# Row loads of the decay issued by GpSimd, and the first 500 places of a written order replaced

## The chip, the cores and the metric

The kernel runs on one NeuronCore of a Trainium2 chip. The metric is the device time of one execution in microseconds, as the median of several executions. TensorE multiplies matrices into PSUM; VectorE, ScalarE and GpSimd work on SBUF (VectorE and ScalarE on PSUM too); SyncE, called SP, only issues DMA. In the profile these engines are PE (with PEld, its weight loads), DVE, ACT, POOL and SP.

## The reference

A forgetting attention, whose result is the input of a gated feed-forward block with a convolution:

```python
# q, k, v: (8 batches, 8 heads, 576, 64); f: (8, 8, 576)
scores = np.matmul(q, k.transpose(0, 1, 3, 2)) / np.sqrt(64)
cum = np.cumsum(np.log(np.clip(f, 1e-4, 1.0)), axis=-1)
scores = np.where(causal, -1e9, scores + cum[:, :, :, None] - cum[:, :, None, :])
attn = softmax(scores)
x = matmul(attn, v)                     # brought to (8, 576, 512)
h = np.maximum(x @ w_in, 0.0)           # w_in: 512 x 1024
conv_out[s] = sum over k of conv_w[k] * h[s + k - 1]     # three taps along the sequence
out = (h / (1 + np.exp(-conv_out))) @ w_out              # w_out: 1024 x 512
```

## The kernel before

The attention is worked in 16 half batches of four heads (`hb` 0 to 15), each of two pairs of heads (`i` = 2 hb + p). The feed-forward block is worked by batch (`b` 0 to 7) and by eight slices of 128 hidden channels (`ff`). The program is a set of small steps, each with a name, an engine or a choice of engines, the steps it needs and the buffers that it takes and gives (`add`). They are issued in the order that the string `ORDER` (line 18) writes out, one place for each step; `@ACT` and the like after a name choose the engine. Each engine runs its own steps in that order, and PSUM buffers (four of them, `ps`) go round in that order as well. The names:

- `dca`, `dcl`, `dcs`, `dck`: the decay `f` is clipped, its logarithm taken (ScalarE), summed by a scan and scaled into the rows `kc` (VectorE). `ki` (line 278, `decay_image`): three DMA transfers write `kc` to an image in DRAM.
- `cw`, `cwt`: the convolution weights are turned on TensorE and made into ratios by seven small steps on VectorE.
- `ld`, `tp`, `cl` of half batches 0 and 1: q (side 0) and k (side 1) are loaded plainly, turned by TensorE (`turn_qk`, line 162, nine transposes) and copied from PSUM into the buffers `qk` by ScalarE or VectorE (`turned_qk`, line 168). Later half batches come with a transposing DMA of SP (`q2.0`, `q2.1` and so on, `load_qk`, line 177); for half batches 2 to 7 VectorE then clamps rows in place (`cl2.0` and so on, line 184).
- `rw1` to `rw7` (line 200, `rows_of`): two DMA transfers bring rows of the image into the q and k buffers of a half batch, so that the score product adds the decay. Half batch 0 adds it by extra matmuls instead (`by_matmul`); half batches 8 to 15 take it by `fi` (`fill`).
- `v`, `va`: v is loaded by SP in five parts for each batch and cast to 16 bits by POOL, ACT or DVE (`va2.0`: parts 0 to 3; `va2.1`: the last; lines 219 and 221).
- `sd`, `so`, `st`: score products on TensorE, of the diagonal blocks of a pair, of the blocks off the diagonal for one head, of the last 64 places for a half batch (line 314). `ed`, `eo`, `et`: their exponentials on ScalarE (lines 355, 372, 334). `sd`, `so` and `st` need the half batch's row loads.
- `pv`: the product with v on TensorE in two parts (lines 391 and 396), needing all exponentials and the cast v. `n`, `m`: reciprocal and scaling on VectorE (lines 405 and 407). `t`, `tx`: the result is turned on TensorE (line 416) and copied (line 419).
- `f`: product with `w_in` (line 431); `r`: relu on ScalarE (442); `c`, `d`: convolution on VectorE (448, 450); `a`: tanh on ScalarE (453); `g`: gate on VectorE (460); `o`: product with `w_out` (476); `e`, `s`: copy out and store. `wi`, `wo` and `wic`, `woc` load and cast the weights (line 520).

A DMA that SP issues waits in SP's order for what it needs, and all later ones behind it. Before the change `ki` and `rw1`, `rw2`, `rw3`, `rw6`, `rw7` are issued by SP and `rw4`, `rw5` by ScalarE.

Of the kernel before, what the change touches and what calls it, by code (L numbers as in the profile page):

```python
# [21 lines left out]
class Plan:  # L22
# [34 lines left out]
def kernel(  # L57
# [11 lines left out]
    nc = tc.nc  # L69
# [5 lines left out]
    BH = B * H  # L75
# [24 lines left out]
    image = dpool.tile([4, 2, BH, S], BF16, name="image")  # L100
# [45 lines left out]
    add = plan.add  # L146
# [53 lines left out]
    def rows_of(hb, e="SP"):  # L200
        dma = {"SP": nc.sync, "ACT": nc.scalar}[e].dma_start
        h0 = 2 * PAIRS if hb == 0 else 0
        c = slice(hb * HH + h0, (hb + 1) * HH)
        dma(even_rows(hb, 0, 1, h0 * S, HS), image[0:1, 0, c, :].rearrange("j h s -> j (h s)"))
        dma(even_rows(hb, 1, 2, HS + h0 * S, 2 * HS), image[1:3, 1, c, :].rearrange("j h s -> j (h s)"))
# [73 lines left out]
    def decay_image(e):  # L279
        for j, a, h in ((0, 0, 0), (1, 1, 0), (2, 1, 1)):  # L280
            {"SP": nc.sync, "ACT": nc.scalar}[e].dma_start(image[j, a], kc[BH * h:BH * (h + 1)])
# [256 lines left out]
    for hb in range(NHB):
        b = hb // 2
        was = hb - RING  # L540
        old = [f"st{was}"] + [f"sd{2 * was + y}" for y in range(2)] + [
            f"so{2 * was + y}.{s}" for y in range(2) for s in range(2)] if was >= 0 else []
        if hb < NPL:
            parts = [(p, side) for p in range(2) for side in range(2)]
            loads = [(p, 1, side) for p, side in parts] if hb == 0 else [(0, 2, side) for side in range(2)]
            add(f"ld{hb}", "SP", [], lambda: None, take=["he"])
            got = {}
            for p0, np, side in loads:
                n = add(f"ld{hb}.{p0}.{side}", "SP", [], lambda hb=hb, side=side, p0=p0, np=np: load_plain(hb, side, p0, np),
                        behind=[f"ld{hb}"])  # L550
                got.update({(p, side): n for p in range(p0, p0 + np)})
            for p, side in parts:
                add(f"tp{hb}.{p}.{side}", "PE", [got[p, side]], lambda hb=hb, p=p, side=side: turn_qk(hb, p, side),
                    take=["ps"], give=[("he", f"ld{hb}")] if (p, side) == (1, 1) else [],
                    behind=[f"tp{hb}.{x}.{y}" for x, y in parts] [:2 * p + side])
                add(f"cl{hb}.{p}.{side}", "DVE/ACT", [f"tp{hb}.{p}.{side}"] + old,
                    lambda e, hb=hb, p=p, side=side: turned_qk(hb, p, side, e), give=[("ps", f"tp{hb}.{p}.{side}")])
            if hb == 0:
                ready = [["dck"] + [f"cl0.{p}.{side}" for side in range(2)] for p in range(2)]
                if PAIRS < 2:  # L560
                    add("rw0", "SP", ["cl0.1.0", "cl0.1.1", "ki"] + ([] if PAIRS else ["cl0.0.0", "cl0.0.1"]), lambda: rows_of(0))
                    ready = [ready[p] if p < PAIRS else ["rw0"] for p in range(2)]
            else:
                add(f"rw{hb}", "ACT/SP", [f"cl{hb}.{p}.{side}" for p, side in parts] + ["ki"], lambda e, hb=hb: rows_of(hb, e))
                ready = [[f"rw{hb}"]] * 2
        else:
            for side in range(2):
                add(f"q{hb}.{side}", "SP", old, lambda hb=hb, side=side: load_qk(hb, 0, 4, side))
            if hb < NCL:
                for side in range(2):  # L570
                    add(f"cl{hb}.{side}", "DVE", [f"q{hb}.{side}"], lambda hb=hb, side=side: clamp(hb, 0, 4, side))
                add(f"rw{hb}", "ACT/SP", [f"cl{hb}.{side}" for side in range(2)] + ["ki"], lambda e, hb=hb: rows_of(hb, e))
                ready = [[f"rw{hb}"]] * 2
            else:
                add(f"fi{hb}", "SP", [f"q{hb}.0", f"q{hb}.1", "zc", "ki"], lambda hb=hb: fill(hb))
                ready = [[f"fi{hb}"]] * 2
# [43 lines left out]
    for b in range(B):  # L620
# [72 lines left out]
```

## Time and profile before

| | |
|---|---|
| median of three runs | 245.96 us (245.56 to 246.7) |
| the profiled execution | 247.66 us, of which the span of the trace is 245.9 |
| TensorE busy | 229.1 us (93%) |
| VectorE busy | 205.7 us (84%) |
| ScalarE busy | 207.2 us (84%) |
| GpSimd busy | 52.6 us (21%) |
| DMA | 49.68 MB |

The profile is of one execution. Its page has the busy time of the engines, the span in 40 slices, the DMA queues, the chain of waits that ended last, and the costliest groups of instructions. A row of the timeline has the start in us, the length, the engine, the line of the code, the operation, what it writes and reads, the count of instructions put together, and in brackets the idle time before it and what ended that. A matmul's end is modelled, so that rows of TensorE overlap; the distance from start to start is the step's price. Idle time of an engine that sets nothing costs nothing.

### The profile page before, as it was taken

How to read it: one execution, taken by the hardware profiler on the slowest of the kernel's cores; microseconds unless marked ns; L12 is line 12 of the kernel's file. 1: busy time of each engine (PE TensorE's matmuls, PEld its weight loads, DVE VectorE, ACT ScalarE, POOL GpSimd, SP SyncE). 2: the span in 40 equal slices, each digit the busy share in tenths (PEclk: the TensorE clock that was granted, in tenths of full speed). 3: DMA queues.
4: the chain of work that ended last, by engine and by line, in shares of the span. 5: the costliest groups of instructions: out<-in, count | busy, mean ns of one | idle time of the engine just before them, and what ended most of it. 6: DMA issues, size and time to landing. Idle time of an engine off the chain costs nothing.

```text
span 245.9 us, 6391 instructions
## 1 busy us (share of the span) xinstructions
PE 229.1 (93%) x2627; PEld 146.5 (60%) x2627; DVE 205.7 (84%) x323; ACT 207.2 (84%) x278; POOL 52.6 (21%) x77
## 2 busy tenths in 40 slices
PE   0899899959999999999999999999999999999992
PEld 0778676537655776666556865685576557444440
DVE  5626329899999899999999988996999889999951
ACT  2748695999999889999999999999988997698452
POOL 8020430004240030004130481156303131000000
PEclk9999999999999999999999999999999999999999
DMA  6999799999999899999989999929999780551426
GB/s 202 329 154 231 242 189 206 219 201 325 225 203 191 198 196 219 234 301 212 234 248 249 177 191 283 263 48 187 272 245 197 185 192 4 129 176 50 171 87 213
DMA packets 120280, 49.68 MB, mean 202 GB/s; under 512 B 109863, under 2 KB 110375, under 8 KB 120251
## 3 DMA queue, kind: packets, MB, share of 16 engines
q1 hardware_dynamic: 120073, 48.94, 89.1%
q8 instruction: 20, 0.33, 0.6%
q10 hardware_dynamic: 178, 0.34, 0.5%
q14 instruction: 9, 0.07, 0.1%
HBM read 21.11 MB, written 10.17 MB: 127 GB/s over the span
## 4 chain that ended last, share of the span: by engine, by line
PE 79%; DVE 7%; DMA 5%; ACT 5%; issue 1%; SPq 1%; ACTq 0%; DVEq 0%
PE ps L476 25%; PE ps L431 24%; PE ps L314 15%; PE ps L391 7%; DMA qk<-image 3%; DMA u<-in_f_dram 2%; PE ps L396 2%; PE ps L416 2%; PE ps L322 2%; ACT qk L172 2%; DVE xm L407 2%; DVE u L448 1%; DVE u L450 1%; PE ps L317 1%; PE ps L319 1%
## 5 line engine op out<-in xcount | busy, mean ns | idle before, releaser
L431 PE MATMUL ps<-xt,w_in_f 128*128 128x512 f16 (+1 forms) x512 | 70.1, 287 | 0.4 <-DVE xt L419 0.4
L372 ACT ACTIVATE pp<-ps 128x1024 f16<-128x1024 f32 x64 | 64.6, 1030 | 4.1 <-PE ps L314 2.3
L476 PE MATMUL ps<-w_out_f,hg 128*128 128x512 f16 x288 | 66.8, 380 | 0.0
L314 PE MATMUL ps<-qk 128*128 128x128 bf16 (+2 forms) x576 | 64.8, 242 | 1.3 <-ACT pp L355 0.7
L448 DVE SCALAR_TENSOR_TENSOR u<-ht,cwt 128x576 f32<-128x576 f16 x64 | 54.0, 860 | 3.9 <-ACT ht L442 3.6
L453 ACT ACTIVATE hg<-u,cw 128x576 f16<-128x576 f32 x64 | 48.6, 781 | 6.1 <-DVE u L450 6.0
L450 DVE SCALAR_TENSOR_TENSOR u<-ht,cwt,u 128x576 f32<-128x576 f16 x64 | 52.9, 841 | 0.5
L431 PEld LDWEIGHTS <-w_in_f 128*128 128x128 f16 x512 | 34.3, 98 | 28.7 <-issue 0.5
L314 PEld LDWEIGHTS <-qk 128*128 128x128 bf16 x576 | 39.7, 98 | 19.5 <-issue 3.5
L442 ACT ACTIVATE ht<-ps 128x576 f16<-128x576 f32 x64 | 40.9, 661 | 6.4 <-PE ps L431 3.0
L476 PEld LDWEIGHTS <-hg 128*128 128x128 f16 x288 | 26.9, 98 | 28.9
L460 DVE SCALAR_TENSOR_TENSOR hg<-hg,ht 128x576 f16<-128x576 f16 x51 | 38.8, 773 | 0.5 <-ACT hg L453 0.5
L358 POOL TENSOR_SCALAR_AFFINE_SELECT pp<-pd 128x1024 f16<-128x1024 f32 x16 | 19.7, 1245 | 54.2 <-ACT pd L355 54.2
L391 PE MATMUL ps<-va,pp 128*128 128x65 f16 x640 | 24.8, 193 | 1.7 <-DVE va L219 1.7
L391 PEld LDWEIGHTS <-pp 128*128 128x128 f16 x640 | 22.6, 97 | 4.2 <-DVE va L219 2.0
L407 DVE TENSOR_TENSOR xm<-ps,rc 128x896 f16<-128x896 f32 (+1 forms) x32 | 23.9, 752 | 0.5
L355 ACT ACTIVATE pp<-ps 128x1024 f16<-128x1024 f32 x16 | 16.5, 1034 | 5.8 <-PE ps L314 3.3
L355 ACT ACTIVATE pd<-ps 128x1024 f32<-128x1024 f32 x16 | 16.2, 1023 | 1.2 <-PE ps L314 0.5
L219 POOL CAST va<-vf 128x1024 f16<-128x1024 f32 x8 | 9.9, 1233 | 32.6 <-DVE u L448 18.3
L322 PE MATMUL ps<-mask,ident 128*128 128x512 bf16 (+1 forms) x40 | 14.8, 370 | 1.4 <-ACT pp L372 0.8
L405 DVE RECIPROCAL rc<-ps 128x14 f32<-128x14 f32 (+1 forms) x32 | 6.7, 209 | 10.1 <-PE ps L396 4.9
L481 ACT COPY ob<-ps 128x1024 f32<-128x1024 f32 (+1 forms) x14 | 12.9, 918 | 0.3 <-issue 0.2
(83 smaller groups left out, 180.2 us busy)
## 6 DMA issues: line engine op xcount, KB each, us to landing
vf<-in_v_dram SPq DMA_DIRECT2D x32, 256.0 KB
out_dram<-ob SPq DMA_DIRECT2D x14, 512.0 KB
qk<-blank SPq DMA_DIRECT2D x8, 432.0 KB
ob<-in_moe_w_in_dram SPq DMA_DIRECT2D x4, 512.0 KB
ob<-in_moe_w_out_dram SPq DMA_DIRECT2D x4, 512.0 KB
out_dram<-ob SPq DMA_DIRECT2D x6, 256.0 KB
vf<-in_v_dram SPq DMA_DIRECT2D x8, 128.0 KB
qk<-blank SPq DMA_DIRECT2D x8, 108.0 KB
```

Of the source, the lines that this page charges most:

```text
L314: nc.tensor.matmul(o, tk[:, h * S + k0:h * S + k0 + 128], tq[:, h * S + q0:h * S + q0 + n], start=first, stop=last and not by_matmul(hb, h))
L355: nc.scalar.activation(o, ps_of(f"sd{i}").rearrange("p (s c) -> p s c", s=2), AF.Exp, scale=SCALE)
L372: nc.scalar.activation(pair(i)[:, s, 512:1536], ps_of(f"so{i}.{s}"), AF.Exp, scale=SCALE)
L391: nc.tensor.matmul(ps[:, c:c + D + 1], block(hb, h, m, n), va[:, h, m, 0:D + 1], start=(m == 0), stop=(m == n))
L407: nc.vector.tensor_tensor(xm[:, CUT * D * u:CUT * D * u + nj * k * D].rearrange("p (j x d) -> p j x d", x=k, d=D), got[:, :, :, 0:D], r.un ...
L431: nc.tensor.matmul(ps[:, t0:t1], w_in_f16[:, cc, 128 * ff:128 * (ff + 1)], xt[:, cc // 2, x:x + t1 - t0], start=(cc == 0), stop=(cc == NCC ...
L442: nc.scalar.activation(ht_of(b, ff)[:, 2:2 + S], ps_of(f"f{b}.{ff}")[:, 0:S], AF.Relu, scale=1.0 if (b, ff) in LATE else 0.5)
L448: nc.vector.scalar_tensor_tensor(u, ht[:, 1:1 + S], cwt[:, ff, 0:1], ht[:, 2:2 + S], op0=ALU.mult, op1=ALU.add)
L450: nc.vector.scalar_tensor_tensor(u, ht[:, 3:3 + S], cwt[:, ff, 1:2], u, op0=ALU.mult, op1=ALU.add)
L453: nc.scalar.activation(hg_of(b, ff), u_t[slot[f"c{b}.{ff}", "u"]], AF.Sigmoid if (b, ff) in LATE else AF.Tanh, scale=cw[:, ff, 1:2])
L460: nc.vector.scalar_tensor_tensor(hv, hv, 1.0, ht_of(b, ff)[:, 2:2 + S], op0=ALU.add, op1=ALU.mult)
L476: nc.tensor.matmul(ps[:, 512 * (c % 2):512 * (c % 2 + 1)], w, w_out_f16[:, ff, :], start=(ff == 0), stop=(ff == NFF - 1))
```

## The change

`rows_of` and `decay_image` may be issued by GpSimd as well, and the first 500 of the 1054 places of the order are others; the last 554 are as they were. The same 1054 steps are done. In the new order

- `ki` is issued by ScalarE and `rw1` to `rw7` by GpSimd;
- other steps change engine: `cl0.1.0` and `cl1.0.0` go from ScalarE to VectorE and `cl1.0.1` the other way; `wic1`, `wic2`, `wic3` from GpSimd to ScalarE and `woc2` from GpSimd to VectorE; `tx1` from VectorE to ScalarE; the value casts `va1.0`, `va6.0` and `va6.1` from GpSimd to VectorE, `va4.0` and `va5.1` from ScalarE to VectorE, `va3.0`, `va7.1` and `va8.0` from ScalarE to GpSimd, `va7.0` from VectorE to GpSimd; the copy out `e1.1` from ScalarE to VectorE;
- `q4.1` comes behind the loads of batch 1's values (`v1`), as `q4.0` did;
- the four transposes of half batch 1 come directly behind `sd0`, and `pv0.0` comes behind half batch 1's first scores; the convolution ratios `cwt` come ahead of the scan `dcs`.

The order is one line in the file; here it is broken, and shown up to `f1.2`:

```diff
--- before.py
+++ after.py
 ORDER = """
-dca cw ld0 ld1 ld0.0.0 tp0.0.0 dcl ld0.1.0 ld0.0.1 tp0.0.1 tp0.1.0 v0.0 ld0.1.1 ld1.0.1 ld1.0.0 dcs
-dck v0.1 v0.2 v0.3 v0.4 va0.0@POOL ki@SP va0.1@POOL q2.1 cl0.0.0@ACT cl0.0.1@ACT cl0.1.0@ACT tp0.1.1
-q2.0 cwt sd0 ed0 cl0.1.1@DVE wi1 wic1@POOL so0.1 eo0.1 tp1.0.0 so0.0 eo0.0 tp1.0.1 cl1.0.0@ACT
-cl1.0.1@DVE sd1 ed1 va1.0@POOL va1.1@DVE tp1.1.0 tp1.1.1 cl1.1.1@ACT so1.1 eo1.1 so1.0 st0 eo1.0
-pv0.0 et0 cl1.1.0@DVE rw1@SP sd2 ed2 so2.1 eo2.1 st1 wi0 so2.0 sd3 wi2 wic0@POOL wi3 et1 eo2.0 cl2.0
-cl2.1 rw2@SP n0.0 m0.0 q3.0 q3.1 so3.1 wic2@POOL ed3 so3.0 eo3.0 pv0.1 sd5 n0.1 eo3.1 m0.1 ed5 pv1.0
-so5.1 eo5.1 t0 pv1.1 n1.0 sd4 m1.0 tx0@DVE n1.1 m1.1 t1 q4.1 v1.0 v1.4 tx1@DVE f0.0 so4.1 f0.1 v1.1
-ed4 cl3.0 r0.0 cl3.1 c0.0 so5.0 f0.2 d0.0 cl4.1 r0.1 eo4.1 r0.2 c0.2 h0 so4.0 eo5.0 a0.0 eo4.0 c0.1
-wic3@POOL rw3@SP f0.3 d0.2 f0.4 f0.5 sd6 r0.3 r0.4 a0.2 so6.1 c0.3 c0.4 v1.3 v1.2 ed6 g0.0 r0.5 d0.3
-d0.4 q4.0 va2.0@DVE eo6.1 sd7 so7.0 pv2.0 so6.0 g0.2 eo7.0 q5.0 va3.0@ACT a0.4 f0.6 q5.1 d0.1 ed7
-eo6.0 n2.0 cl4.0 c0.5 g0.4 va2.1@POOL va3.1@ACT st3 st2 m2.0 wo3 d0.5 rw4@ACT wo1 et2 wo0 so7.1 v2.0
-et3 cl5.0 r0.6 c0.6 eo7.1 a0.1 pv2.1 n2.1 d0.6 m2.1 v2.3 v2.4 f0.7 pv3.0 t2 r0.7 n3.0 c0.7 m3.0 a0.5
-pv3.1 woc3@POOL woc1@POOL tx2@ACT n3.1 a0.6 m3.1 sd9 t3 so9.1 st4 ed9 a0.3 et4 eo9.1 sd8 cl5.1
-tx3@DVE rw5@ACT woc0@POOL ed8 f1.0 so9.0 v2.1 v2.2 d0.7 g0.3 f1.1 wo2 g0.6 g0.5 g0.1 eo9.0 so8.1
-a0.7 q6.0 va5.0@POOL q6.1 r1.1 g0.7 f1.2
...
+ld0 ld1 dca ld0.0.0 ld0.1.0 ld0.0.1 cw dcl v0.0 tp0.0.0 tp0.0.1 cl0.0.0@ACT cwt ld0.1.1 tp0.1.0
+ld1.0.1 ld1.0.0 v0.1 cl0.0.1@ACT dcs tp0.1.1 v0.2 dck v0.3 sd0 tp1.0.0 cl0.1.1@DVE va0.0@POOL v0.4
+q2.1 tp1.0.1 q2.0 cl0.1.0@DVE wi1 tp1.1.0 wi0 ki@ACT ed0 wi2 cl1.0.0@DVE tp1.1.1 cl1.1.0@DVE sd1 wi3
+cl1.0.1@ACT cl1.1.1@ACT so0.1 va0.1@POOL cl2.1 rw1@POOL so1.0 va1.0@DVE ed1 cl2.0 so1.1 st0 eo0.1
+so0.0 eo1.0 eo1.1 st1 et0 q3.0 eo0.0 q3.1 v1.0 v1.4 sd2 sd3 so3.0 ed2 et1 ed3 rw2@POOL so2.1 pv0.0
+va1.1@DVE so2.0 eo3.0 eo2.1 n0.0 pv0.1 n0.1 eo2.0 so3.1 m0.0 m0.1 wic2@ACT sd5 eo3.1 ed5 pv1.0 pv1.1
+n1.0 m1.0 wic1@ACT t0 n1.1 wic0@POOL so5.1 m1.1 wic3@ACT tx0@DVE t1 cl3.0 sd4 tx1@ACT f0.0 so5.0
+eo5.1 f0.1 r0.0 ed4 eo5.0 c0.0 d0.0 h0 r0.1 f0.2 a0.0 cl3.1 rw3@POOL f0.3 so4.0 so4.1 c0.1 r0.2 c0.2
+g0.0 eo4.0 f0.4 r0.3 d0.2 v1.1 v1.3 v1.2 q4.1 q4.0 q5.0 q5.1 a0.2 eo4.1 f0.5 d0.1 va2.0@DVE f0.6
+r0.6 g0.2 r0.4 r0.5 pv2.0 c0.3 st2 et2 cl4.1 n2.0 wo3 wo1 wo0 v2.0 sd6 v2.3 c0.6 so6.0 v2.4 a0.1
+va2.1@POOL sd7 ed6 m2.0 c0.4 va3.0@POOL cl4.0 eo6.0 so6.1 eo6.1 so7.0 pv2.1 d0.6 so7.1 eo7.0 v2.1
+f0.7 a0.6 v2.2 n2.1 g0.1 rw4@POOL d0.4 m2.1 d0.3 cl5.0 va3.1@ACT eo7.1 st3 ed7 pv3.0 a0.3 wo2 r0.7
+q6.0 q6.1 cl5.1 t2 et3 n3.0 tx2@ACT pv3.1 m3.0 n3.1 sd8 m3.1 q7.0 t3 c0.5 a0.4 tx3@DVE ed8 so8.0
+c0.7 sd9 d0.5 d0.7 q7.1 v3.0 v3.1 eo8.0 g0.4 so9.1 st4 f1.0 ed9 g0.3 a0.5 g0.5 g0.6 et4 a0.7
+rw5@POOL f1.1 f1.2
...
@@ -198,7 +198,7 @@
-        dma = {"SP": nc.sync, "ACT": nc.scalar}[e].dma_start
+        dma = {"SP": nc.sync, "ACT": nc.scalar, "POOL": nc.gpsimd}[e].dma_start
...
@@ -278,7 +278,7 @@
-            {"SP": nc.sync, "ACT": nc.scalar}[e].dma_start(image[j, a], kc[BH * h:BH * (h + 1)])
+            {"SP": nc.sync, "ACT": nc.scalar, "POOL": nc.gpsimd}[e].dma_start(image[j, a], kc[BH * h:BH * (h + 1)])
...
@@ -529,7 +529,7 @@
-    add("ki", "ACT/SP", ["dck"], decay_image)
+    add("ki", "ACT/SP/POOL", ["dck"], decay_image)
...
@@ -561,7 +561,7 @@
-                add(f"rw{hb}", "ACT/SP", [f"cl{hb}.{p}.{side}" for p, side in parts] + ["ki"], lambda e, hb=hb: rows_of(hb, e))
+                add(f"rw{hb}", "ACT/SP/POOL", [f"cl{hb}.{p}.{side}" for p, side in parts] + ["ki"], lambda e, hb=hb: rows_of(hb, e))
...
@@ -569,7 +569,7 @@
-                add(f"rw{hb}", "ACT/SP", [f"cl{hb}.{side}" for side in range(2)] + ["ki"], lambda e, hb=hb: rows_of(hb, e))
+                add(f"rw{hb}", "ACT/SP/POOL", [f"cl{hb}.{side}" for side in range(2)] + ["ki"], lambda e, hb=hb: rows_of(hb, e))
```

2 lines of the change are left out of this document (1 added, 1 removed).

## The prediction

> **What bounds the kernel now.** I read the page's busy line and queues first, then the busy time of each engine by stretches, then the waits of TensorE, then the chain of waits, and last the rows of single instructions.
>
> ```profile
> span 245.9 us, 6391 instructions
> PE 229.1 (93%) x2627; PEld 146.5 (60%) x2627; DVE 205.7 (84%) x323; ACT 207.2 (84%) x278; POOL 52.6 (21%) x77
> q1 hardware_dynamic: 120073, 48.94, 89.1%
> q10 hardware_dynamic: 178, 0.34, 0.5%
> ```
>
> TensorE is busy 93% of the span. All DMA goes through the queues of SP (q1) and ScalarE (q10): no row shows a transfer issued by GpSimd. The stretches (length, then busy us of PE, PEld, DVE, ACT and POOL with counts, granted clock, DMA share, GB/s):
>
> ```profile
> 15.00:25.00 10.00, 10.00 (x118) 8.03 (x116) 4.24 (x5) 7.42 (x7) 1.37 (x2) 1.00 0.98 196
> 25.00:45.00 20.00, 18.72 (x270) 13.30 (x268) 10.76 (x18) 14.56 (x19) 5.51 (x6) 1.00 1.03 210
> 45.00:62.00 17.00, 13.63 (x220) 9.74 (x218) 16.40 (x27) 16.36 (x24) 3.33 (x4) 1.00 1.17 255
> 62.00:100.00 38.00, 37.84 (x447) 24.34 (x446) 36.93 (x54) 36.10 (x51) 5.53 (x5) 1.00 1.06 206
> 100.00:160.00 60.00, 60.00 (x684) 37.54 (x683) 56.40 (x81) 58.46 (x81) 15.68 (x15) 1.00 1.09 240
> ```
>
> From 62 us on TensorE idles 0.16 us in 98, so no relief of ScalarE, VectorE or a queue there can be worth anything: only a lead that TensorE has won by 62 us is carried to the end. Open to the change are 1.28 us of idle in 25 to 45 and 3.37 in 45 to 62, where VectorE (16.40 of 17) and ScalarE (16.36) are full. TensorE's largest and its smallest wait from 25 to 62 us (waiter, released by, us, times, longest):
>
> ```profile
> PE ps L391 <- DVE va L219: 1.7, 1, 1.7
> ...
> PE ps L314 <- DMA qk<-image: 0.2, 1, 0.2
> ```
>
> The largest is pv2.0, the value product of half batch 2, waiting for the cast of its values on VectorE. Row loads, which the change is named for, cost TensorE only 0.2 us, although one of them is slow in the chain of waits (start, us, what):
>
> ```profile
> 24.46 0.69 SPq L205
> ...
> 26.74 0.25 SPq L204
> 27.10 6.63 DMA qk<-image
> ```
>
> This is rw2: from the first issue at 26.74 to the release at 33.73 it takes 7.0 us behind the weight loads in SP's queue.
>
> **The change part by part.** The sum is made on the profiled execution, 247.66 us, whose span is 245.9, so 1.8 lie around it; the median of the runs shown is 245.96, 1.7 lower. The sum gives a difference, which I take off the median.
>
> *Issue moved.* The three image transfers go from SP to ScalarE, the row pairs rw1 to rw7 from SP (five) and ScalarE (two) to GpSimd. Rows of their issue (count; min/median/max ns):
>
> ```profile
> L281 SPq DMA_DIRECT2D image<-kc x3: 539/540/595, 13.8 to 15.1; - x3
> L205 SPq DMA_DIRECT2D qk<-image x5: 593/597/690, 24.5 to 86.6; - x5
> L204 ACTq DMA_DIRECT2D qk<-image x2: 219/226/234, 53.5 to 63.1; - x2
> L205 ACTq DMA_DIRECT2D qk<-image x2: 612/637/662, 53.8 to 63.4; - x2
> ```
>
> SP loses 3 x 0.54 and five pairs of about 0.98, with the waits before them, so its later loads are issued sooner; but the DMA share is 0.98 to 1.17 in every stretch from 15 us, so they land little sooner: 0. ScalarE's 1.6 us of image issue falls behind the second copy out of PSUM and ahead of ed0, which starts at 16.12 after 2.46 idle:
>
> ```profile
> 16.12 1.02 ACT L355 ACTIVATE pp<-ps 128x1024 f16<-128x1024 f32 x1 [2.46 <-PE ps L319]
> 22.43 1.48 DVE L174 TENSOR_SCALAR qk<-ps,lim 128x1152 uint16<-128x1152 uint16 x1 [0.68 <-PE ps L166]
> 26.63 1.16 PE L391 MATMUL ps<-va,pp 128*128 128x65 f16 x32
> ...
> 27.84 0.39 PE L314 MATMUL ps<-qk 128*128 128x128 bf16 x4
> ```
>
> So it is hidden, the more as one copy ahead of it (cl0.1.0) goes to VectorE; without that gap it would hold up ed0 behind it by 1.6. ScalarE also loses two row pairs, about 0.86 us each, of issue.
>
> *A GpSimd row pair* is not in the trace. Lower bound: rw1 on SP, whose second part is issued at 24.46, is read at 27.84 without a wait, so a pair can take under 4 us. Upper bound: rw2's 7.0. I take 5, nearer the low end, since GpSimd's queue has no bulk loads ahead. Slack: half batch 1's four transposes now come before so0.1. They end at about 18.1 (ed0's start, 16.1, and four of about 0.5), and two VectorE copies of 1.48 from 16.7 make its rows ready at 19.8, against 23.9 (22.43 and 1.48) before. First use is st1, when TensorE is through the same steps that it ended at 26.6 before (pv0.0's first row): slack 6.8. By the walk below rw3 has 6.3 (clamp cl3.1 ends at 43.8, sd6 starts near 50) and rw4 about 6; rw6 and rw7 come out alike. At 5 us all are hidden: 0. GpSimd itself, 3.33 busy of 17, has room for the issue and for the extra value casts. Behind rw3's wait for its clamps stand va2.1 and va3.0, read by pv2.1 and pv3.0 over 6 us later, behind rw6 and rw7 the casts of half batch 7, later still.
>
> [...]
>
> *The order around 27 to 62.* TensorE's step prices, from starts of neighbouring rows:
>
> ```profile
> 57.14 1.15 PE L431 MATMUL ps<-xt,w_in_f 128*128 128x512 f16 x8
> 58.13 1.16 PE L391 MATMUL ps<-va,pp 128*128 128x65 f16 x32
> 59.13 0.66 PE L416 MATMUL ps<-ident,xm 128*128 128x128 f16 x9
> 59.63 0.41 PE L391 MATMUL ps<-va,pp 128*128 128x65 f16 x8
> 60.41 0.39 PE L322 MATMUL ps<-mask,ident 128*128 128x512 bf16 x1
> ...
> 62.20 0.60 PE L314 MATMUL ps<-qk 128*128 128x64 bf16 x4
> 62.64 0.27 PE L322 MATMUL ps<-mask,ident 128*128 128x256 bf16 x1
> 62.87 0.38 PE L322 MATMUL ps<-mask,ident 128*128 128x512 bf16 x1
> ...
> 63.75 1.14 PE L431 MATMUL ps<-xt,w_in_f 128*128 128x512 f16 x8
> ```
>
> FFN step f 0.99, pv first part 1.00, turn t 0.50, pv second part 0.78, so 0.44, st 0.23, sd 0.88; f1.0 starts at 63.75. The second half of f0.0, whose four pairs of matmuls take half of 0.99 and so end at 40.06, then VectorE, and pv2.0 with what releases it:
>
> ```profile
> 39.57 0.65 PE L431 MATMUL ps<-xt,w_in_f 128*128 128x512 f16 x4 [0.36 <-DVE xt L419]
> ...
> 39.43 1.69 DVE L186 TENSOR_SCALAR qk<-qk,lim 128x2304 uint16<-128x2304 uint16 x2
> ...
> 49.04 1.54 DVE L450 SCALAR_TENSOR_TENSOR u<-ht,cwt,u 128x576 f32<-128x576 f16 x2
> 50.50 0.69 DVE L219 CAST va<-vf 128x1024 f16<-128x1024 f32 x1
> ...
> 51.24 0.42 PE L391 MATMUL ps<-va,pp 128*128 128x65 f16 x8 [1.67 <-DVE va L219]
> ```
>
> ScalarE (start to next start: an exponential 0.90, a relu 0.55; a tanh 0.67, its row's 0.77 less the 0.10 by which a relu's row overlaps the next start):
>
> ```profile
> 56.68 1.05 ACT L372 ACTIVATE pp<-ps 128x1024 f16<-128x1024 f32 x1
> 57.58 0.80 ACT L453 ACTIVATE hg<-u,cw 128x576 f16<-128x576 f32 x1
> 58.39 0.65 ACT L442 ACTIVATE ht<-ps 128x576 f16<-128x576 f32 x1
> 58.94 0.77 ACT L453 ACTIVATE hg<-u,cw 128x576 f16<-128x576 f32 x1
> ```
>
> (1) *Up to the end of f0.0* the same TensorE steps are done. The new order puts three weight casts (wic1 to 3) and tx1 on ScalarE; at 0.90 each, like an exponential of the same 128x1024, that is 3.6 us, against 14.56 busy of 20: they fit, but sit in the chain eo3.1, pv1, m1, t1, tx1. My walk has f0.0 end at 40.1 to 40.4 against 40.06: +0.1.
>
> (2) *From there to pv2.0.* Before: 11.18 us (to 51.24) for 5 f, 5 so, 2 sd = 8.9, so 2.3 lost. VectorE had three clamps (0.8, from 1.69 for two) and ten conv or gate steps (0.73, from 1.46 for two) ahead of the value cast, 9.7 us. Now two clamps and seven steps: 6.7, counted from tx0 with a wait for r0.0, so the cast ends near 48.5. It is no longer alone: ScalarE must do 5 exponentials, 4 relus, 2 tanh = 8.0 after tx1 (39.8) and waits some 0.6 for d0.2, so eo4.1 ends at 48.4. TensorE does 6 f and 3 so (7.3) in 8.2 us: 0.9 lost. Gain 1.4. Loading half batch 4's q and k behind the values only takes q4.1's transfer out of their way; the values' landing did not decide before, VectorE's queue did.
>
> (3) *From pv2.0 to f1.0.* Before: 12.51 us for 10.3 of steps, 2.2 lost. Now 12.4 of steps (sd6, sd7, so6.1, so7.0 and so8.0 have moved in) and ScalarE leads: 6 exponentials, 3 relus, 2 tanh and some 0.7 of small ones are 9.1 after eo4.1, so ed7 ends and pv3.0 starts at 57.5; 5.7 of steps follow, f1.0 at 63.2. Lost 2.3: +0.1. (va3.0, now on GpSimd, is no longer among ScalarE's steps.)
>
> Sum: +0.1 - 1.4 + 0.1 = -1.2. Check: f1.0 0.55 earlier with 0.44 (so8.0) more done, -1.0. After f1.0 nothing is added or lost on a full TensorE. -1.2 off 245.96 is 244.8; its own range is 243.9 to 245.6 (a walk of 30 rounded steps: 0.8 either way).
>
> **Rivals.**
> *GpSimd's row pairs land late (slower).* Place: st1, sd6, sd8, sd12; it decides once ready to landed exceeds 6 to 6.8 us, and turns the sum positive past 7. [...] Against: the bounds from rows, 4 to 7. At 7.5 us: 0.7 + 1.2 + 0.5 + 1.3 = 3.7 lost, less 1.2: 248.5. [...]
>
> *ScalarE takes the place of VectorE (same).* It is 16.36 of 17 busy, and by the walk it ends both stretches; if the casts put on it ahead of f0.0 delay it by 1 us, the gain is gone: 245.8.
>
> *The waits close (faster).* If ScalarE's walk is 1.2 us too long (in (3) four waits of about 0.5 hang on it), 1.2 more is won: 243.6. Bound: all 3.37 idle of 45 to 62 gone, 242.6.
>
> *Row loads were the bound* and the change wins rw2's 6.63: against it stands the 0.2 us of TensorE's wait; 2 in 100.
>
> **How the numbers follow.** Forecast 0.48, late row pairs 0.21, ScalarE instead 0.17, waits close 0.14 (the row-load case in it). Half a per cent, 1.23 us, is about what a measurement tells from no change. Faster: 0.14 and 0.27 of the forecast's 0.48, 0.41. Same: the other 0.21 and 0.16 of ScalarE's case, 0.37. Slower: 0.21 and 0.01, 0.22. The range runs from the closed waits, 242.9, into the late row pairs, 248.0.
>
> **What would show it.** Right: the wait of pv2.0 for a VectorE cast is gone or under 1 us and an exponential ends it; f1.0's first matmul comes near 63.2; the row loads of GpSimd release nothing on TensorE; TensorE is still full from 64 us. Wrong: waits of st1, sd6, sd8 or sd12 for qk<-image of a us or more each; GpSimd DMA instructions of over 2 us; new idle of TensorE after 64 us, where I count none; or f0.0 ending later than 41, which would be the ScalarE case.

## The result: one per cent slower

| | before | after |
|---|---|---|
| median | 246.63 us (20 executions, 245.5 to 250.11) | 249.05 us (20 executions, 247.61 to 251.52) |
| the profiled execution | 247.66 us, span 245.9 | 248.26 us, span 246.5 |
| ratio after / before | | 1.0105 (95% interval 1.0083 to 1.0127) |

The change costs 2.4 us; 244.8 was forecast, and 249.05 lies outside the range. Here and below, ratios leave out executions more than 1.5% above the fastest of their kernel; medians have all. The two profiled executions are only 0.6 apart: the one before lies 1.0 above its median, the one after 0.8 below.

From the page after, the busy line, and the queue that is new:

```profile
span 246.5 us, 6424 instructions
PE 227.7 (92%) x2627; PEld 145.3 (59%) x2627; DVE 208.0 (84%) x329; ACT 205.8 (83%) x275; POOL 57.2 (23%) x88
...
q0 software_dynamic: 448, 0.10, 0.3%
```

The stretches after (columns as in the prediction: length, then busy us of PE, PEld, DVE, ACT, POOL, granted clock, DMA share, GB/s):

```profile
25.00:45.00 20.00, 19.37 (x273) 13.48 (x271) 10.45 (x17) 18.25 (x22) 4.40 (x6) 1.00 1.14 231
45.00:62.00 17.00, 13.41 (x220) 9.89 (x217) 15.77 (x27) 15.15 (x22) 5.57 (x7) 1.00 1.13 237
62.00:100.00 38.00, 38.00 (x448) 24.42 (x447) 37.26 (x56) 36.14 (x50) 6.40 (x7) 1.00 1.09 209
...
122.00:135.00 13.00, 12.15 (x110) 6.73 (x109) 12.93 (x19) 11.13 (x17) 1.71 (x2) 1.00 1.12 250
```

and the last of them before:

```profile
122.00:135.00 13.00, 13.00 (x123) 7.58 (x122) 12.91 (x17) 12.75 (x19) 3.40 (x3) 1.00 0.99 250
```

25 to 45 us is better than before (0.63 idle where it was 1.28), 45 to 62 no better (3.59 where it was 3.37), and there is new idle of 0.85 from 122 to 135 us, where there was none. TensorE's largest waits after 20 us in the new kernel:

```profile
PE ps L391 <- ACT pp L372: 1.8, 1, 1.8
PE ps L314 <- DMA qk<-image: 0.9, 1, 0.9
PE ps L314 <- ACT ht L442: 0.8, 2, 0.6
```

The wait of pv2.0 is as long as before (1.67), with ScalarE at its end. These rows of the timeline after show how it comes about:

```profile
42.86 1.60 POOL L219 CAST va<-vf 128x1024 f16<-128x1024 f32 x1
43.48 1.59 DVE L460 SCALAR_TENSOR_TENSOR hg<-hg,ht 128x576 f16<-128x576 f16 x1
45.84 0.78 ACT L453 ACTIVATE hg<-u,cw 128x576 f16<-128x576 f32 x1 [1.74 <-DVE u L450]
...
47.57 1.15 PE L391 MATMUL ps<-va,pp 128*128 128x65 f16 x32 [1.78 <-ACT pp L372]
```

GpSimd casts va3.0, a step that the change took from ScalarE; the gate g0.0, which lies beside it on VectorE, takes 1.59 us (0.72 to 0.76 where GpSimd does nothing beside it). The tanh a0.2 waits 1.74 for VectorE's d0.2, with the exponential eo4.1 (46.52) and pv2.0 behind it. Two of the row loads are late as well. rw2 is issued from 24.39 and sd5 waits for it at 31.87; rw4 is issued from 53.20 and sd8 waits for it at 59.76:

```profile
24.39 0.51 POOL L204 DMA_DIRECT2D qk<-image  x1 [4.38 <-DVE va L221]
...
29.67 0.24 DVE L405 RECIPROCAL rc<-ps 128x14 f32<-128x14 f32 x1 [5.38 <-PE ps L391]
31.87 0.38 PE L322 MATMUL ps<-mask,ident 128*128 128x512 bf16 x1 [0.32 <-DMA qk<-image]
...
53.20 0.51 POOL L204 DMA_DIRECT2D qk<-image  x1 [8.73 <-PE ps L396]
...
59.76 0.40 PE L314 MATMUL ps<-qk 128*128 128x128 bf16 x4 [0.87 <-DMA qk<-image]
```

### The profile page after: what moved, and what is told of

It reads as the page before. It is cut to its first block, busy times and chain, and to the rows that moved or that the text cites. A ratio compares the mean times of both kernels' runs of the same rounds, so it can differ in the third digit from the quotient of the medians.

```text
span 246.5 us, 6424 instructions
## 1 busy us (share of the span) xinstructions
PE 227.7 (92%) x2627; PEld 145.3 (59%) x2627; DVE 208.0 (84%) x329; ACT 205.8 (83%) x275; POOL 57.2 (23%) x88
## 4 chain that ended last, share of the span: by engine, by line
PE 76%; ACT 7%; DMA 7%; DVE 6%; issue 2%; ACTq 1%; DVEq 0%
PE ps L476 24%; PE ps L431 20%; PE ps L314 14%; PE ps L391 6%; ACT pp L372 3%; DMA qk<-image 2%; PE ps L396 2%; DMA pd<-in_moe_conv_w_dram 2%; PE ps L322 2%; DMA qk<-in_k_dram 2%; PE ps L416 2%; PE ps L166 2%; DVE u L448 2%; DVE hg L460 2%; ACT ht L442 1%
## 5 line engine op out<-in xcount | busy, mean ns | idle before, releaser
L431 PE MATMUL ps<-xt,w_in_f 128*128 128x512 f16 (+1 forms) x512 | 68.8, 286 | 0.5 <-ACT pp L372 0.3
L314 PE MATMUL ps<-qk 128*128 128x128 bf16 (+2 forms) x576 | 63.4, 240 | 1.9 <-DMA qk<-image 0.9
L450 DVE SCALAR_TENSOR_TENSOR u<-ht,cwt,u 128x576 f32<-128x576 f16 x64 | 52.2, 831 | 0.6
L391 PE MATMUL ps<-va,pp 128*128 128x65 f16 x640 | 25.3, 193 | 2.1 <-ACT pp L372 1.8
L391 PEld LDWEIGHTS <-pp 128*128 128x128 f16 x640 | 23.1, 97 | 5.7 <-DVE va L219 1.7
L219 POOL CAST va<-vf 128x1024 f16<-128x1024 f32 x9 | 12.4, 1372 | 15.7 <-DMA vf<-in_v_dram 11.7
L322 PE MATMUL ps<-mask,ident 128*128 128x512 bf16 (+1 forms) x40 | 14.3, 362 | 0.8 <-DMA qk<-image 0.3
L186 DVE TENSOR_SCALAR qk<-qk,lim 128x2304 uint16<-128x2304 uint16 x12 | 10.2, 864 | 3.2 <-DMA qk<-in_k_dram 1.9
```

The costliest lines, as they stand in the source:

```text
L314: nc.tensor.matmul(o, tk[:, h * S + k0:h * S + k0 + 128], tq[:, h * S + q0:h * S + q0 + n], start=first, stop=last and not by_matmul(hb, h))
L391: nc.tensor.matmul(ps[:, c:c + D + 1], block(hb, h, m, n), va[:, h, m, 0:D + 1], start=(m == 0), stop=(m == n))
L431: nc.tensor.matmul(ps[:, t0:t1], w_in_f16[:, cc, 128 * ff:128 * (ff + 1)], xt[:, cc // 2, x:x + t1 - t0], start=(cc == 0), stop=(cc == NCC ...
L450: nc.vector.scalar_tensor_tensor(u, ht[:, 3:3 + S], cwt[:, ff, 1:2], u, op0=ALU.mult, op1=ALU.add)
```

## The experiments

Two theories at first. Q: transfers issued by GpSimd cost time by themselves. V: the order costs, because VectorE is behind in it. In the diffs the one long line of the order is broken, and only the neighbours of a step are shown.

### Each part of the change alone

The new order with the old engines for the rows:

```diff
-rw1@POOL ... rw2@POOL ... rw3@POOL ... rw4@POOL ... rw5@POOL ... rw6@POOL rw7@POOL
+rw1@SP ... rw2@SP ... rw3@SP ... rw4@ACT ... rw5@ACT ... rw6@SP rw7@SP
```

> The changed kernel with the row loads back on the engines of before (rw4, rw5 by ScalarE, the other five by SyncE), all at their new places; ki stays on ScalarE. Theory Q (a transfer issued by GpSimd costs time by itself: 0.9 us more behind the last store in the trace, and rows that land up to 7.2 us after their issue): about 0.3 us under the kernel before, so 246.3, and the stretch behind the last store is as before. Theory V (the new order's lead on TensorE is lost where VectorE sets the pace, and the row loads do nothing): as the changed kernel, 249.0. Q with SyncE held up by the waits of the rows: 247 to 248.

Measured: 272.81 us, ratio 1.109 (1.1059 to 1.1122). Neither theory had this. Its timeline, the row loads in SP's queue (rw3's two transfers, then rw6's first) and who waited:

```profile
42.82 0.24 SPq L204 DMA_DIRECT2D qk<-image  x1
46.99 0.56 SPq L205 DMA_DIRECT2D qk<-image  x1
...
106.31 0.24 SPq L204 DMA_DIRECT2D qk<-image  x1
...
108.62 0.61 PE L314 MATMUL ps<-qk 128*128 128x128 bf16 x4 [7.92 <-DMA qk<-image]
```

In the new order SP's queue has the loads at places where a row load that waits for its clamps holds up those behind it, and rw6 comes through only at 106.31 (79.39 before). The places and the engine belong together.

The other part: the old order, with the rows issued by GpSimd.

```diff
-rw1@SP ... rw2@SP ... rw3@SP ... rw4@ACT ... rw5@ACT ... rw6@SP ... rw7@SP
+rw1@POOL ... rw2@POOL ... rw3@POOL ... rw4@POOL ... rw5@POOL ... rw6@POOL ... rw7@POOL
```

> The order of before with rw1 to rw7 issued by GpSimd, ki on SyncE as it was. Theory Q: 0.9 us at the end and some late rows, so 247.5 to 249, 1 to 2.4 us above before. Theory V: the order is what costs, so this is as before, 246.6, within 0.5 us.

Measured: 258.43 us, 1.050 (1.0473 to 1.0527). Its timeline:

```profile
26.19 1.04 POOL L520 CAST w_in_f<-ob 128x1024 f16<-128x1024 f32 x1 [8.34 <-DMA ob<-in_moe_w_in_dram]
...
28.16 0.64 POOL L204 DMA_DIRECT2D qk<-image  x1
...
34.23 0.61 PE L314 MATMUL ps<-qk 128*128 128x128 bf16 x4 [8.35 <-DMA qk<-image]
```

Here rw1 stands behind a weight cast that waits 8.34 us for its load, and TensorE waits 8.35 us in one place. The change takes such casts off GpSimd, so that its rows don't stand behind them. Then one row alone:

```diff
-rw7@SP
+rw7@POOL
```

> The kernel before with rw7 alone issued by GpSimd (first read over 6 us after it is ready). Theory Q with a fixed price for having such a queue at all: 0.9 us above before, 247.5, all of it outside the stretch in which TensorE works. Theory Q by late rows only: as before, 246.6. Theory V: as before.

Measured: 251.06 us, 1.0144 (1.0093 to 1.0195), with executions from 247.69 to 251.68. My "over 6 us" counted from when the row is ready, but on GpSimd rw7 comes behind the cast va6.0 and is issued only at 89.89 (86.17 on SP before, in a trace that started 2.0 us later); from there to the matmul that waited for it are 5.9 us:

```profile
88.90 1.04 POOL L219 CAST va<-vf 128x1024 f16<-128x1024 f32 x1 [18.48 <-DVE u L450]
89.89 0.65 POOL L204 DMA_DIRECT2D qk<-image  x1
...
95.81 0.40 PE L314 MATMUL ps<-qk 128*128 128x128 bf16 x4 [3.17 <-DMA qk<-image]
```

Its fixed price can't be read from the time, but from the trace: from the issue of the last store to the end it takes 3.73 us, where the kernel before takes 3.50. So one pair costs 0.2 there and not 0.9. And theory V's own test, VectorE relieved in the changed kernel:

```diff
-va6.0@DVE ... va6.1@DVE ... e1.1@DVE
+va6.0@POOL ... va6.1@POOL ... e1.1@ACT
```

> The changed kernel with three steps taken from VectorE again: e1.1 on ScalarE, va6.0 and va6.1 on GpSimd, as they were before the change; 1.2 + 0.7 + 0.3 = 2.2 us less on VectorE ahead of 126 us. Theory V: the lead of 1.76 us at 122 us lives on, 1.0 to 1.5 us under the changed kernel, 247.5 to 248. Theory Q: VectorE's work does not matter, 249.0 as the changed kernel.

Measured: 249.28 us, 1.011 (1.0077 to 1.0143): nothing won. From 122 to 135 us TensorE still idles, now also behind an exponential on ScalarE, where e1.1 had gone. VectorE's part there did shrink: a relu that waits for a gate (shown below for the changed kernel, 1.49 us) waits 0.94, but TensorE waits 0.64 for that exponential. So this run shifts the wait and doesn't decide on theory V.

### Without the row loads, and both kernels again

```diff
-        dma(even_rows(hb, 0, 1, h0 * S, HS), image[0:1, 0, c, :].rearrange("j h s -> j (h s)"))
-        dma(even_rows(hb, 1, 2, HS + h0 * S, 2 * HS), image[1:3, 1, c, :].rearrange("j h s -> j (h s)"))
+        return
```

> The changed kernel without the row loads rw1 to rw7: half batches 1 to 7 are scored without the decay, so the output is not the reference's; the order, and ki on ScalarE, stay. Theory Q (the rows from GpSimd cost: late landings, TensorE at half clock for 3.4 us after a long wait, 0.4 us more of closing waits for the queue's semaphores at the end): it falls by 1.5 to 2.5 us to 246.5 to 247.5, and its executions lie closer together. Theory V (the order itself is slower, as VectorE is behind): only the 0.4 at the end goes, 248.6.

> The kernel before without rw1 to rw7 (half batches 1 to 7 scored without the decay). It tells what the rows cost in the old order, and the difference to the changed kernel without them is what the order alone is worth. Theory Q: the order alone is the gain predicted, so this is 0.5 to 1.2 us slower than the changed kernel without rows; rows cost the old order 0.2 us of TensorE's wait, 246.0. Theory V: 1 us or more faster than the changed kernel without rows.

Both kernels leave out the transfers of every row load, and with them the decay that these bring. Measured: new order 247.17 us (245.99 to 247.42), ratio to the kernel before 1.0019 (0.9994 to 1.0045); old order 246.21 us, 1.0006 (0.9978 to 1.0034). So the rows cost the new order 1.9 us by the medians (249.05 less 247.17), 2.1 by the ratios, and the old one nothing that the times show (without rows its last store's landing is followed by 0.5 us more of waiting at the end, which can hide as much). Without rows the new order's twelve executions lie within 1.4 us, with them the twelve of the next runs within 4.1. The new order alone brings no gain: 1.0 us behind by the medians, level within the intervals. Counted from the start of ed0, its trace without rows leads the old order's by 1.18 us at o1.4 (a product with w_out, the last step of the changed part) and by 0.02 two such products on, so the lead is lost there without any row. The rows do cost, as theory Q has it, but these two runs don't show that GpSimd's issue is what makes them cost; the part of it that the order alone is the predicted gain falls.

The kernels themselves again, for second traces:

> The kernel before, unchanged, for a second trace. In the first one TensorE was granted its full clock only from 16.65 us on, in the others from 11.6 to 13.4. If that start is chance, the full clock comes near 12 here, ed0 starts near 14 and the span is 1.0 to 1.5 us shorter than 245.9; the sum of the prediction was then made on an execution with a late start. If it belongs to the order, 16.6 and 245.9 again.

> The changed kernel, unchanged, for a second trace. Theory Q: the wait of sd5 or sd8 for the rows is longer than in the first trace (0.32 and 0.87 us) where the span is longer than 246.5, and a window of half clock follows a long one. Theory V: rows as in the first trace, and the loss again between 122 and 133 us.

Measured: before 246.43 us (0.999), after 249.75 us (1.0107, 1.0068 to 1.0147; 12 executions, six of them over 250). These two traces happen to start alike, which the first two did not (ed0 at 16.12 and 14.70): the late start of the first trace before was chance. Before, second trace:

```profile
14.55 1.02 ACT L355 ACTIVATE pp<-ps 128x1024 f16<-128x1024 f32 x1 [1.36 <-PE ps L319]
...
62.37 1.14 PE L431 MATMUL ps<-xt,w_in_f 128*128 128x512 f16 x8
...
122.87 1.89 PE L476 MATMUL ps<-w_out_f,hg 128*128 128x512 f16 x8
...
130.25 1.89 PE L476 MATMUL ps<-w_out_f,hg 128*128 128x512 f16 x8
```

and after, second trace:

```profile
14.55 1.02 ACT L355 ACTIVATE pp<-ps 128x1024 f16<-128x1024 f32 x1 [2.72 <-PE ps L319]
...
62.33 3.84 PE L431 MATMUL ps<-xt,w_in_f 128*128 128x512 f16 x30
...
121.69 1.89 PE L476 MATMUL ps<-w_out_f,hg 128*128 128x512 f16 x8
...
130.12 0.28 PE L314 MATMUL ps<-qk 128*128 128x64 bf16 x4 [0.61 <-ACT ht L442]
130.24 1.89 PE L476 MATMUL ps<-w_out_f,hg 128*128 128x512 f16 x8
```

Step for step: f1.0 at the same time (with so8.0, 0.44, more done); o1.4 1.18 us earlier; o2.1, the next product but one, eight us on, at the same time. The lead is won and gone again by 130 us. A relu waits for a gate on VectorE to free its buffer, and TensorE waits for the relus:

```profile
ACT ht L442 <- DVE hg L460: 1.5, 1, 1.5
```

VectorE itself passes 130 us 0.63 later than before (gates at 130.17 and 129.54). The last stores are issued 0.25 later, and the span ends 1.2 later (246.0 against 244.8): another 0.95 lies behind the last stores, and it is there in the first pair of traces too. The rows of SP's waits at the end of the program, before and after:

```profile
L688 SPq EVENT_SEMAPHORE  x8: 17/28/28, 242.8 to 245.9; - x8
```

```profile
L688 SPq EVENT_SEMAPHORE  x12: 17/28/28, 242.5 to 246.5; - x12
```

With the seven pairs on GpSimd there are twelve closing waits in place of eight. Behind the one for the last store's landing come seven others, where one came before; at 0.06 us each that is 0.36 of the 0.42 by which the way from the last packet to the end is longer (1.69 in place of 1.27). The old order with its rows on GpSimd has the same 1.70. The other half us is the last store's landing (2.75 us from its issue, 2.23 before). GpSimd's queue alone isn't what makes it longer: the new order with its rows off GpSimd takes 2.76 too. What does stays open.

### The half clock

In the traces with VectorE relieved and with rw7 alone on GpSimd there were stretches in which TensorE's granted clock was 0.5, each of them 3.41 us long (32.59 to 36.00 and 96.97 to 100.38). The question is what goes ahead of them. Theory H: a late rw2, at sd5. Two runs for it:

```diff
     def rows_of(hb, e="SP"):
+        if hb == 2:
+            return
```

> The changed kernel without rw2 alone (half batch 2 is scored without the decay); the other six row loads stay on GpSimd. Theory H (in some executions rw2 lands so late that TensorE, waiting at sd5, falls to half clock for 3.4 us; that is the 2 to 3 us between the fastest and the slowest executions): no execution with a mean granted clock under 0.991 and none over 249.5, median 248.0. Rival (all row loads share the cost, rw4 at sd8 as much as rw2): median 248.7, and executions over 250 remain.

```diff
-et0 ... eo0.0 ... ed3 rw2@POOL so2.1
+et0 ... rw2@ACT eo0.0 ... ed3 so2.1
```

> The changed kernel with rw2 issued by ScalarE ahead of the exponential eo0.0, near 25.6 us; the other six stay on GpSimd. Theory H: the rows land by 30 us, no half clock at sd5, executions over 250 vanish; ScalarE's 0.86 us of issue delays its exponentials, so 248.0 to 248.6. Rival (issue by any engine lands as late, the transfer being slow behind the bulk loads): as the changed kernel, 249 to 249.8, half clock as often.

Measured: without rw2 249.24 us (six executions, 247.29 to 251.56; 1.0111, 1.0070 to 1.0153), and rw2 by ScalarE 249.75 us (1.013, 1.008 to 1.018). Both far from 248.0; theory H falls as the main cause. Without rw2 five of the six executions have a mean clock of 0.995 to 0.998, too high for a stretch of half clock, and a median of 249.04 all the same; so the half clock doesn't make all of the loss. In the second run rw2 was issued from 23.73, and sd5 waited for it still:

```profile
23.73 0.24 ACTq L204 DMA_DIRECT2D qk<-image  x1
...
32.03 0.38 PE L314 MATMUL ps<-qk 128*128 128x128 bf16 x4 [0.67 <-DVE xm L407]
```

The row names VectorE, whose last step had ended at 31.61. In the trace TensorE's weight loads for this matmul wait for the two semaphores of rw2's transfers, and the last signal comes at 31.94. So rw2 landed 8.2 us after ScalarE issued it; from GpSimd it took 7.4 (24.39 to 31.83), from SP 7.0 before. The rival written down ahead of this run holds at this place: the pair is as late from any of the three engines, so GpSimd isn't what makes it late.

A half clock was there as well, behind pv2.0. Four pairs of neighbouring stretches of 3.41 us, each from another execution; the count starts where TensorE first had its full clock (in the second trace before from 13.20 to 50.74, 11 stretches of 3.413; with VectorE relieved from 12.11 to 32.59, 6; with rw7 alone on GpSimd from 11.64 to 96.97, 25). VectorE relieved (sd5 waits 1.86 us in the first of the two):

```profile
29.18:32.59 3.41, 1.33 (x25) 0.65 (x21) 1.49 (x3) 3.14 (x4) 0.00 (x0) 1.00 1.30 112
32.59:36.00 3.41, 3.24 (x46) 2.99 (x47) 0.01 (x1) 1.77 (x2) 0.00 (x0) 0.50 1.13 256
```

rw2 by ScalarE (pv2.0 waits 1.90 in the first):

```profile
44.88:48.29 3.41, 1.51 (x36) 1.18 (x35) 3.41 (x7) 2.64 (x4) 0.00 (x0) 1.00 1.20 243
48.29:51.71 3.42, 3.42 (x29) 2.31 (x26) 3.42 (x7) 2.63 (x5) 0.00 (x0) 0.50 1.21 144
```

the kernel before, second trace (pv2.0 waits 1.67 in the first):

```profile
47.33:50.74 3.41, 1.44 (x32) 1.05 (x31) 3.41 (x6) 3.11 (x5) 0.00 (x0) 1.00 1.15 175
50.74:54.15 3.41, 3.41 (x27) 1.90 (x23) 3.31 (x6) 3.32 (x5) 0.00 (x0) 0.50 1.18 240
```

and the kernel before, first trace, where the same wait of 1.67 lies across the border of two stretches:

```profile
47.37:50.78 3.41, 1.90 (x18) 1.08 (x15) 3.41 (x6) 3.11 (x5) 0.00 (x0) 1.00 1.19 181
50.78:54.19 3.41, 2.58 (x44) 1.89 (x45) 3.41 (x7) 3.41 (x6) 0.00 (x0) 1.00 1.09 219
```

Stretches with 1.16 (rw7 alone on GpSimd, from 93.56), 1.33, 1.44 and 1.51 us of TensorE's work were followed by one at half clock, and one with 1.71 (51.98 to 55.40 in the last run below); stretches with 1.50 (after, second trace, from 44.02), 1.52 (VectorE relieved, from 46.24) and 1.90 (before, first trace) were not, so these traces show no sharp edge. In the old order the wait of 1.67 us was followed by a half clock where it lay within one stretch, and not where it lay across a border. It is not always paid. From pv2.0 to f1.0 the kernel before takes 12.51 us without the half clock and 12.46 with it (49.91 to 62.37): VectorE and ScalarE, busy 16.26 and 16.07 of 17 us from 45 to 62 in the second trace, set the pace there. The new order takes 15.34 and 15.17 without it, and 16.89 with it (47.39 to 64.28, rw2 by ScalarE): in the new order sd6, sd7, so6.1 and so7.0 lie behind pv2.0, ahead of which they were before, and ScalarE's exponentials wait for them. That the half clock at pv2.0 is what costs the new order is theory W, tested below.

### The wait of pv2.0 taken away

First in both orders without late rows in play:

```diff
-v1.1 v1.3 v1.2 q4.1 ... va2.1@POOL sd7 ed6 m2.0 c0.4 va3.0@POOL cl4.0
+v1.1 v1.3 v1.2 va3.0@ACT q4.1 ... va2.1@POOL sd7 ed6 m2.0 c0.4 cl4.0
```

> The changed kernel without the row loads (half batches 1 to 7 scored without the decay), and the value cast va3.0 on ScalarE, ahead of the tanh a0.2, where ScalarE waited 1.74 us for VectorE. In the traces of the new order a VectorE step takes 1.6 to 1.8 in place of 0.8 us while GpSimd casts va3.0 at 43, and the tanh, the exponential eo4.1 and pv2.0 wait behind it. Theory S (that stretch is most of pv2.0's wait): the wait falls from 1.5 to 0.7. If a lead won there is carried to the end: 246.4; if VectorE sets the pace at 122 to 135 us in any case: the wait falls, and the time stays 247.2.

```diff
-c0.4 v1.3 v1.2 ed6 g0.0 r0.5 d0.3 d0.4 q4.0 va2.0@DVE eo6.1
+c0.4 v1.3 v1.2 ed6 va2.0@DVE g0.0 r0.5 d0.3 d0.4 q4.0 eo6.1
```

> The kernel before with the value cast va2.0 three steps earlier on VectorE (ahead of the gate g0.0 and the convolutions d0.3, d0.4). It takes away alone the wait that the prediction's step (2) was about: pv2.0 then starts near 49.5 - 50 us in place of 51.24 by the first trace's times. As the prediction has it (a lead won by 62 us is carried to the end): 245.0, 1.3 us faster. Rival (VectorE and ScalarE, both full from 45 to 62 us, set f1.0, and the wait goes to a later step): 246.3, within 0.3.

Measured: 246.71 us for the first, ratio 1.0029 (1.0008 to 1.0050), no better than without the move (1.0019); and 247.6 us for the second, 1.008 (1.0051 to 1.0109), slower than either side had. In the first the wait falls from 1.49 to 0.94, with no step of VectorE lengthened ahead of it (without the move two convolutions there took 2.32), and a wait of 0.86 comes in its place at 63.53 (line numbers are one lower in this kernel):

```profile
46.24 1.15 PE L390 MATMUL ps<-va,pp 128*128 128x65 f16 x32 [0.94 <-ACT pp L371]
...
63.53 2.34 PE L430 MATMUL ps<-xt,w_in_f 128*128 128x512 f16 x16 [0.86 <-ACT pt L333]
```

In the second the wait of pv2.0 falls from 1.67 to 0.96, now for ScalarE. Counted from the start of ed0 pv2.0 comes only 0.2 to 0.4 us earlier (34.9, where it was 35.1 and 35.4), and more than that is lost behind it: the gate and the two convolutions that the cast was put ahead of come later, ScalarE's tanhs and exponentials with them, and TensorE waits for those:

```profile
49.71 1.15 PE L391 MATMUL ps<-va,pp 128*128 128x65 f16 x32 [0.96 <-ACT ht L442]
...
54.05 0.27 PE L322 MATMUL ps<-mask,ident 128*128 128x256 bf16 x1 [1.38 <-ACT pp L355]
...
66.34 0.60 PE L314 MATMUL ps<-qk 128*128 128x64 bf16 x4 [0.80 <-ACT pp L355]
```

Then the changed kernel itself, rows on GpSimd, with the same move of va3.0 to ScalarE:

> The changed kernel, all row loads on GpSimd, with the value cast va3.0 on ScalarE ahead of the tanh a0.2. Theory W (TensorE's clock is granted in stretches of 3.41 us counted from its first full clock; a stretch in which TensorE is busy for under some 0.45 is followed by one at half clock; pv2.0's wait of 1.8 to 1.9 us brings the new order to that edge, by chance of where the stretches lie, and behind pv2.0 half clock costs 1.9): the wait falls to 1.0 to 1.2, that half clock vanishes, median 248.0, only the executions with a long wait at sd5 remain above 250. Rival (the half clock is not what separates the executions): the median stays at 249 or above.

Measured: 247.8 us (1.0053, 1.0031 to 1.0074), against 1.0105 and 1.0107 of the changed kernel. pv2.0 waits 0.94. Ten of twelve executions lie between 246.59 and 248.58; two, at 252.36 and 253.01 with a mean granted clock of 0.98, remain, and this trace shows sd5 waiting 1.48 for rw2. The move that brought nothing without the rows takes off 1.3 us (by the ratios) with them. Theory W holds for the executions over 250 us: of the second twelve of the changed kernel these are six, with a mean clock of 0.986 to 0.989, the others have 0.994 to 0.999. One stretch of half clock takes 0.007 off the mean (half of 3.41 in 246 us; the two traces before have 0.999 without and 0.993 with one), so only the six can have had one; with the move two of twelve are left. But W isn't the whole 1.3: of the executions with 0.994 or more the changed kernel's median is 248.1 in these twelve (six) and 248.4 in all 32 (eighteen), and the moved one's 247.4 (nine). So 0.7 to 1.0 us is won without any half clock, and what wins it stays open. Neither trace of the changed kernel itself shows a half clock while TensorE works.

Last, rw4 by ScalarE on top of that:

```diff
-g0.1 rw4@POOL d0.4
+g0.1 rw4@ACT d0.4
```

> The same, with rw4 issued by ScalarE at its place. It prices the two issuers for one row load: from GpSimd rw4's first packet moved 3.6 to 4.4 us after the issue and sd8 waited 0.7 to 0.9. If GpSimd's issue is what is slow: rows of rw4 land within 4 us, sd8 waits for no row, another 0.3 to 0.7 less, 247.5. If the transfer is slow behind the bulk loads: sd8 waits 0.5 or more still, and the time is that of the kernel with the cast moved, plus up to 0.5 for ScalarE's 0.9 us of issue.

Measured: 253.33 us (1.0294, 1.0264 to 1.0324), which neither side had:

```profile
52.65 0.24 ACTq L204 DMA_DIRECT2D qk<-image  x1
56.58 0.68 ACTq L205 DMA_DIRECT2D qk<-image  x1
57.29 0.41 ACT L221 CAST va<-vf 64x256 f16<-64x256 f32 x1 [4.21 <-DMA ob<-in_moe_w_out_dram]
```

ScalarE's second transfer stood 3.7 us until a load of w_out had landed, with a cast and an exponential behind it, and TensorE idled 4.36 us at pv3.0. In the trace that load (issued by SP at 51.42) and this transfer carry the same completion semaphore (the count that tells of a landing), and the transfer waits for it. So this run doesn't price the issuer as it was meant to; what it shows is that here a row load put ScalarE 3.7 us behind a load it has nothing to do with. In the first trace after, the transfers of SP and ScalarE share eight such semaphores, and the 14 of GpSimd have eight others. GpSimd's idle times ahead of its row loads (2.0 us and more) were ended there by TensorE and VectorE, none by such a load; and all eight of its semaphores are among those waited for at the end.

## Why the prediction was wrong

- *What failed first is the sentence that carried the sum to the end, "After f1.0 nothing is added or lost on a full TensorE".* Between two traces that start alike TensorE's lead was 0.48 at f1.0 (0.04 and so8.0; 1.0 was forecast) and 1.18 at 122 us, all but the forecast 1.2; and by 130 us it was gone, in the pair without rows too. That it was near 1.2 once is luck: 0.7 of it came between 62 and 122 us, where nothing was forecast. From 62 us VectorE is nearly as full as TensorE (36.93 of 38 and 56.40 of 60 busy, in rows that the prediction quotes). In the new order it has more to do (208.0 busy against 205.7) and is no earlier. A full engine says that it has no slack, not that it alone sets the pace.
- *Step (1), +0.1:* from ed0 to the end of f0.0 it was 0.5 better (14.70 to 38.14, against 16.12 to 40.06).
- *Step (2), -1.4, failed.* 0.9 us of loss ahead of pv2.0 was forecast, from a ScalarE that waits 0.6 for d0.2. It waited 1.74: GpSimd's cast of va3.0, which I had counted as harmless on GpSimd, lengthened VectorE's gate by 0.86. 2.2 were lost (38.14 to 47.57 for 7.3 of steps), all but the 2.3 of before. The wait of pv2.0, which was to be gone or under 1 us, was 1.78; an exponential ended it, as said.
- *Step (3):* 15.3 us where 14.8 was forecast, 0.87 of it the wait for rw4.
- *f1.0 near 63.2:* it came at 62.91, but with a start 1.42 earlier than in the trace from which it was worked out. It looked right by chance.
- *"At 5 us all are hidden: 0", failed for two pairs.* Single transfers of GpSimd took 3.0 to 7.2 us from issue to landing, 4.4 in the middle, the issue 0.51 to 0.65 each. But a product needs both of a pair: leaving out rw3, whose second waits for a clamp, pairs took 4.1 to 7.4 from the first issue to the second landing. The slack wasn't worked out for rw2 (7.4), and for rw4 (6.5) it was 5.7. In the old order rw4's first product stood 7.1 us behind the issue (53.51 to 60.64) and didn't wait. So the new order uses rw4 sooner; that GpSimd's issue is the dearer one is not shown. A busy VectorE isn't what made rw2 late: from its issue at 24.39 it took 7.5 us to the matmul that waited for it, and VectorE had nothing to do from 24.30 to 29.67.
- *The rivals.* ScalarE's case (245.8) came true up to 62 us, through VectorE. "Late row pairs" (248.5) is nearest in time and partly in cause: the rows cost 1.9, though not through GpSimd's issue at rw2. The range, which ended at 248.0, left out this rival's own time. Of the 1.9 the waits themselves are about 1.2 in the first trace (0.32 and 0.87) and 0.7 in the second; the half clock in a third of the executions (eleven of 32 have a mean clock under 0.99) and the closing waits, neither of which I counted, come on top.
- *Work before and behind.* I costed the queue of GpSimd at its issues only; it also lengthens the closing waits, by 0.36.

Adding up to the 2.4 between the medians: 0.95 behind the last store and 0.25 of TensorE's time, both from the two traces that start alike. The rest, about 1.2, is not seen in a trace: the second one after is the fastest of its twelve executions, 2.0 under their median. The half clock is a part of it, and longer waits for rows may be (sd5 waited 1.48 for rw2 with va3.0 moved, 0.32 in the first trace after); how much each makes stays open. No version tried beats the kernel before.

## What to carry to other kernels

Before a lead on one engine is carried to the end, look in the same rows whether another engine is as full: then the lead is only a wait somewhere later. A wait has to be judged by what follows it too: here waits of 1.67, 1.86 and 1.90 us were followed by 3.41 us of half clock, and other waits of 1.67, 1.78 and 1.90 were not, so several traces and the spread of the times belong to the comparison. And a profile of one execution has its own luck at the start: compare steps from a common event, not from time zero. Last, a late transfer is not its issuer's fault until another issuer has been tried at the same place: here rw2 was as late from each of three engines (7.0, 7.4 and 8.2 us).

## What the runs showed of the hardware

- In three traces a stretch of half clock began 11, 6 and 25 times 3.413 us after TensorE's first full clock (the kernel before, second trace; VectorE relieved; rw7 alone on GpSimd). Five stretches of 3.41 us that a half clock followed had 1.16 to 1.71 us of TensorE's work; others with 1.50, 1.52 and 1.90 were followed by none.
- At va3.0 a GpSimd cast and the VectorE step beside it took 1.60 and 1.59 us in the first trace after, against 1.04 (the cast at 16.01 in the first trace before, with no VectorE step beside it) and 0.75 alone. In the second the cast took 1.05 and a convolution beside it 1.78, against 0.82 alone.
- Two small transfers (rw2) landed 7.0 to 8.2 us after the first was issued, from SP, GpSimd and ScalarE alike. The DMA share meanwhile was 1.06 with SP (before, 26.74 to 33.73) and 1.14 with GpSimd (after, 24.39 to 31.83); with ScalarE it was 1.13 from 25 to 45 us.
